# Between passes 3 and 4 of a two-layer forward and backward kernel: the last wq product in one piece ahead of the w2 rows, and the store of x4 moved to the last pass

## The chip, the cores and the metric

The kernel runs on one core of a Trainium2 chip. The metric is device time of one launch in microseconds (us), the median of several runs. One more execution was recorded by the hardware profiler; times inside the kernel come from that record and count from the start of its span. PE is TensorE (PEld its weight loads), DVE is VectorE, ACT is ScalarE, POOL is GpSimd and SP is SyncE, whose queue issues the loads.

## The reference

One token, width 1024, goes through attention over a cache and a dense layer, twice with the same weights; all gradients of it are wanted as well.

```python
x = A_x
x = x + _A_ref(_layernorm(x, axis=-1), A_k_cache, A_v_cache, A_wq, A_wo)   # 32 heads, 4 cache groups, 65536 keys
x = x + _B_ref(_layernorm(x, axis=-1), B_w1, B_b1, B_w2, B_b2)             # relu(h)^2, inner width 3584
x = x + _A_ref(_layernorm(x, axis=-1), A_k_cache, A_v_cache, A_wq, A_wo)
x = x + _B_ref(_layernorm(x, axis=-1), B_w1, B_b1, B_w2, B_b2)
return x
...
_out, _vjp = jax.vjp(_f, A_x, A_k_cache, A_v_cache, A_wq, A_wo, B_w1, B_b1, B_w2, B_b2)
return (_out0, *[jnp.asarray(_g) for _g in _grads])
```

Names in the kernel: L1 and L3 are the two attention layers, L2 and L4 the dense ones; x4 is the result (out_0), and dx3, dx2, dx1 are the gradients on the way back: dx3 at the input of L4, dx2 at the input of L3, dx1 at the input of L2. dq, dO and so on are those inside the attention; dh2 is the gradient at L2's inner width.

## The kernel before

The caches (67 MB each for K and V) are read in four passes: forward of L1, forward of L3, backward of L3 (dq alone), and the last, which does the backward of L1 and writes the gradients of K and V for both layers. A pass goes by cache group and by blocks of 32 x 128 rows, in a pipeline written out step by step; inside passes 1 to 3 the order of PE, DVE and ACT is the written one (`tc.manual_schedule(engines=ORDERED)`), while in pass 4 and in the stage between passes 3 and 4 a scheduler of the language orders the instructions of each engine when the program is built. SP and POOL are ordered by it everywhere.

All loaded blocks, weight slabs and staged outputs live in one arena of 20 slots of 1 MB. A slot is given when it is free by the kernel's own bookkeeping at build time (`take_one`, `Slot`, `give_slot`); at run time a load waits for the last reader of its slot. Loads stand in one SP queue in order. Around the stage in question seven slots keep V blocks for pass 4 and eight keep softmax weights, so five take turns for the weights.

Small work that belongs to a pass runs as background steps (`Background`): urgent ones, such as the row dots of a further wo or wq product (`g_rowdots`, L598 on DVE and L587 on ACT), and normal ones, the outer products of the weight gradients. Normal steps are paced: by step i of the pass, `total * i / steps` are to be done. Pass 4 has some 150 of them.

Between passes 3 and 4 four products follow each other, each of a weight matrix and a vector that the one before gives:

- wq with dq of L3's last group: 8 rows of slabs in two slots; its sum goes into dn3 (L989), through the backward of the layer norm (`ln_bwd`, L248, with a mean over partitions on PE, L212) into dx2 (L1836);
- w2 with dx2: 28 rows in seven 1 MB slabs; it gives dh2 (`fin_dh2`, L1838);
- w1 with dh2: 8 rows of 3584 in eight slabs of 896 KB; it gives dx1 (`fin_dx1`, L1841);
- wo with dx1: 8 rows in two slabs; it gives dOT of L1's first group (`dO_finish`, L946), with which pass 4 starts.

The class `Rows` does such a product. A row of the matrix, 128 x 1024, goes one of two ways, chosen at build time by the running load of the engines. Either PE transposes it in eight pieces (`front`, L682), DVE or ACT copies it out of PSUM (L164 and L161, with `evac` choosing), and eight matmuls multiply it with the vector (`back`, L714); or, for the jobs marked `mix`, DVE multiplies it with the vector spread over the partitions and sums (L673, "row dot"), once that spread vector is there (`bcast_vec`: L535 turns the vector, L537 copies it, L544 spreads it). Jobs marked `inplace` copy the transposed row back over the slab, so that they hold no buffer; the others have six buffers `wt`. `begin` (L639) is called at the first product of a job and needs its vector.

Along with the w2 rows runs x4: each row is also multiplied with the second dense layer's activation (`side_x4`, L1849: eight matmuls L1851 a row into `ps_x4`). After the last row two adds make x4 (L1856, L1857), and `col_to_dram` (L202) turns it on PE (L205), copies it (L207) and stores it from POOL's queue (L208).

`rows.run` (L760) transposes rows until the buffers are full, does the products of an in-place first job, fills again, and then alternates; the wq job is queued first, the w2 job second.

Of the kernel before, what the change touches and what calls it, by code (L numbers as in the profile page):

```python
# [20 lines left out]
def kernel(  # L21
# [25 lines left out]
    D = A_x.shape[-1]  # L47
    G = A_k_cache.shape[1]
# [3 lines left out]
    HQ = QD // DH  # L52
    R = HQ // G
    F = B_w1.shape[1]
    DC, FC = D // P, F // P
# [44 lines left out]
    def ps_mv(shape, dtype=F32):  # L100
        if PS["pass4"]:
            return ps_tr(shape, dtype)
        return PS["pool"].tile(shape, dtype, name="ps_mv", tag="mv", bufs=1)
# [98 lines left out]
    def col_to_dram(col, n, v1d):  # L202
        nj = n // P
        pt = ps_mv([nj, P], F32)
        nc.tensor.transpose(pt[:, :], col[:, :], ident_f[:, :])  # L205
        rows = tmp.tile([nj, P], BF, name="rows_c", tag="rows_c")
        nc.vector.tensor_copy(out=rows[:], in_=pt[:])  # L207
        nc.gpsimd.dma_start(out=v1d.rearrange("(j p) -> j p", p=P), in_=rows[:])  # L208

    def bcast_sum(src, ncols, mean=False):  # L210
        pt = ps_mv([P, ncols], F32)
        nc.tensor.matmul(pt[:, :], lhsT=(onesd_f if mean else ones_f)[:, :], rhs=src, start=True, stop=True)  # L212
        return pt
# [34 lines left out]
    def ln_bwd(dn, n, rstd, between=lambda: None):  # L248
        st = tmp.tile([P, 2], F32, name="lnb_st")
        nc.vector.reduce_sum(out=st[:, 0:1], in_=dn, axis=AX.X)  # L250
        pr = tmp.tile([P, DC], F32, name="lnb_pr")
        nc.vector.tensor_tensor(out=pr[:], in0=dn, in1=n[:], op=ALU.mult)
        nc.vector.reduce_sum(out=st[:, 1:2], in_=pr[:], axis=AX.X)
        between()
        tot = bcast_sum(st[:], 2, mean=True)
        negm = tmp.tile([P, 2], F32, name="lnb_negm")
        nc.vector.tensor_scalar(out=negm[:], in0=tot[:], scalar1=-1.0, scalar2=None, op0=ALU.mult)
        t = tmp.tile([P, DC], F32, name="lnb_t")
        nc.vector.scalar_tensor_tensor(out=t[:], in0=n[:], scalar=negm[:, 1:2], in1=dn, op0=ALU.mult, op1=ALU.add)  # L259
        dx = tmp.tile([P, DC], F32, name="lnb_dx")  # L260
        nc.vector.tensor_scalar(out=dx[:], in0=t[:], scalar1=negm[:, 0:1], scalar2=rstd[:, 0:1], op0=ALU.add, op1=ALU.mult)  # L261
        return dx
# [173 lines left out]
    def d_cols(ap, nb):  # L436
        return ap[:, nb * P:(nb + 1) * P]
# [4 lines left out]
    def f_rows_of(W):  # L442
        return W.rearrange("(s p j) n -> p s j n", p=P, j=4)

    def slabs(name, load, nk, kper, ncols, ahead=1, flat=False):
        pend = deque()
        ks = deque(range(0, nk, kper))

        def fetch():
            k = ks.popleft()  # L450
            i = None
            if ks and flat and NOW["wide"] and not odd_one():
                i = take_pair()
            if i is None:
                kn = min(kper, nk - k)
                sl = Slot(name)
            else:
                kn = min(2 * kper, nk - k)
                ks.popleft()
                sl = Slot(name, at=i, both=True)  # L460
            v = sl.t[:, 0:kn * ncols].rearrange("p (k n) -> p k n", n=ncols)
            nc.sync.dma_start(out=v, in_=load(k, kn))
            pend.append((k, kn, sl, v))

        def gen():
            while ks or pend:
                while ks and len(pend) < ahead:
                    fetch()
                k, kn, sl, v = pend.popleft()
                for kk in range(kn):  # L470
                    NOW["slab"] = sl
                    yield k + kk, v[:, kk, :]
                sl.over = True
                if not sl.users:
                    sl.free()
        g = gen()
        g_fetch = [fetch for _ in range(ahead)]
        return g, g_fetch
# [25 lines left out]
    def w2_slabs(ahead=1):  # L504
        v = f_rows_of(B_w2)
        return slabs("s_w2", lambda k, kn: v[:, k // 4, :, :], FC, 4, D, ahead)
# [105 lines left out]
    class Rows:  # L612
# [147 lines left out]
        def run(self):  # L760
            self.fill()
            first = self.queue[0][0] if self.queue else None
            while first is not None and first["inplace"] and self.queue and self.queue[0][0] is first:
                self.back()
            self.fill()
            while self.queue:
                self.back()
                self.fill()
# [5 lines left out]
    DENSE = {}  # L774
# [99 lines left out]
    def new_layer(name, lay):  # L874
        L = dict(name=name)
        for nm in ("qT", "oT", "rZ", "dOT", "dqT"):
            L[nm] = vec.tile([P, HQ], F32, name=name + "_" + nm)
        L["oTb"] = vec.tile([P, HQ], BF, name=name + "_oTb")
        L["qpad"] = vec.tile([P, G, 8, R], BF, name=name + "_qpad")
        L["negm"] = vec.tile([P, G, NSU, R], F32, name=name + "_negm")  # L880
        L["fw"] = vec.tile([P, G, NSU, R], F32, name=name + "_fw")
        L["nd2"] = vec.tile([64, HQ], BF, name=name + "_nd2")
        nc.gpsimd.memset(L["nd2"][:], 0.0)
        return L
# [24 lines left out]
    def gsl(g):  # L909
        return slice(g * R, (g + 1) * R)  # L910
# [73 lines left out]
    def dn_finish(dn, first):  # L984
        def fin(y):
            if first:
                nc.vector.tensor_copy(out=dn[:], in_=y)
            else:
                nc.vector.tensor_tensor(out=dn[:], in0=dn[:], in1=y, op=ALU.add)  # L989
        return fin  # L990
# [7 lines left out]
    ORDERED = {mybir.EngineType.PE, mybir.EngineType.DVE, mybir.EngineType.Activation}  # L998
# [571 lines left out]
    def n_outer(nA, nB, wide=False):  # L1570
        return -(-nB // 8) + nA // 4 + nA * (-(-nB // 8)) if wide else 1 + nA // 4 * 5
# [14 lines left out]
    L1, L3 = new_layer("L1", 0), new_layer("L3", 1)  # L1586
# [31 lines left out]
    lastg = [ITEMS[p][-1][0] for p in range(4)]  # L1618
    firstg = [ITEMS[p][0][0] for p in range(4)]
    PRE = {}  # L1620
# [7 lines left out]
    bg = Background()  # L1628
# [18 lines left out]
    rows = Rows(DENSE["pool"])  # L1647
# [20 lines left out]
    bg = Background()  # L1668
# [86 lines left out]
    rows = Rows(DENSE["pool"])  # L1755
# [59 lines left out]
    bg = Background()  # L1815
    bg.by_group(2, lambda g: g_dO(L3, dx3, g))

    dn3 = vec.tile([P, DC], F32, name="dn3")
# [10 lines left out]
    dx2 = vec.tile([P, DC], F32, name="dx2")  # L1829
# [2 lines left out]

    def fin_dx2(y):
        dn_finish(dn3, False)(y)
        dxn3 = ln_bwd(dn3[:], L3["n"], L3["rstd"])
        nc.vector.tensor_tensor(out=dx2[:], in0=dx3[:], in1=dxn3[:], op=ALU.add)  # L1836

    def fin_dh2(y):  # L1838
# [2 lines left out]
    def fin_dx1(y):  # L1841
        dxn = ln_bwd(y, L2["n"], L2["rstd"])
        nc.vector.tensor_tensor(out=dx1[:], in0=dx2[:], in1=dxn[:], op=ALU.add)
    rows = Rows(DENSE["pool"])
    rows.add(PRE["wq3"], DC, R, lambda: L3["dqT"][:, gsl(lastg[2])], fin_dx2, inplace=True)
    x4 = vec.tile([P, DC], F32, name="x4")
    ps_x4 = ps_acc([P, DC, 64])

    def side_x4(kc, slab):  # L1849
        for nb in range(DC):  # L1850
            nc.tensor.matmul(ps_x4[:, nb, :], lhsT=d_cols(slab, nb), rhs=L4["gb"][:, kc:kc + 1].to_broadcast([P, 64]),  # L1851
                             start=kc == 0 and nb == 0, stop=kc == FC - 1 and nb == DC - 1, skip_group_check=True)
        add_load(pe=DC * 0.03)
        if kc == FC - 1:
            f = tmp.tile([P, DC], F32, name="ffn_f")
            nc.vector.tensor_tensor(out=f[:], in0=ps_x4[:, :, 0], in1=b2c[:], op=ALU.add)  # L1856
            nc.vector.tensor_tensor(out=x4[:], in0=x3[:], in1=f[:], op=ALU.add)  # L1857
            col_to_dram(x4, D, out_0.rearrange("a b d -> (a b d)"))
    rows.add(w2_slabs()[0], FC, DC, lambda: dx2[:], fin_dh2, mix=True, side=side_x4)
    rows.add(w1_slabs()[0], DC, FC, lambda: dh2[:], fin_dx1, cols=f_cols, mix=True)  # L1860
    rows.add(wo_slabs(firstg[3])[0], R, DC, lambda: dx1[:], dO_finish(L1, firstg[3]), inplace=True)
    rows.run()
# [9 lines left out]
    bg = Background()  # L1872
# [1 line left out]
    bg.normal.append(g_outer(bgpool, out_8, FC, DC, [L4["g"], L2["g"]], [gx, dx2], a_f=True))  # L1874
    bg.normal.append(g_outer(bgpool, out_5, HQ, DC, [L3["oT"], L1["oT"]], [dx3, dx1]))
    bg.normal.append(g_outer_wide(bgpool, out_6, DC, FC, [L4["n"], L2["n"]], [dh4, dh2]))
    bg.total = 2 + n_outer(FC, DC) + n_outer(DC, FC, True) + n_outer(HQ, DC) + (G - 1) * n_outer(DC, DC)
    bg.steps = len(ITEMS[3]) - 4
    dn1 = vec.tile([P, DC], F32, name="dn1")

    def g_biases():
        gb2 = tmp.tile([P, DC], F32, name="gb2")
        nc.vector.tensor_tensor(out=gb2[:], in0=gx[:], in1=dx2[:], op=ALU.add)
        col_to_dram(gb2, D, out_9)
        yield
        gb1 = tmp.tile([P, FC], F32, name="gb1")
        nc.vector.tensor_tensor(out=gb1[:], in0=dh4[:], in1=dh2[:], op=ALU.add)
        col_to_dram_f(gb1, F, out_7)
        yield

    bg.normal.append(g_biases())

    def gwq(g):
        return g_outer(bgpool, out_4, DC, R, [L3["n"], L1["n"]], [L3["dqT"][:, gsl(g)], L1["dqT"][:, gsl(g)]], c0=g * 1024)
# [61 lines left out]
```

## Time and profile before

| | us |
|---|---|
| three runs: median (lowest, highest) | 1941.16 (1941.15, 1943.75) |
| profiled execution, span | 1938.1 |
| busy in the span: PE, PEld, DVE, ACT, POOL | 1585.2, 1301.4, 1170.3, 1044.9, 142.2 |
| DMA: 787.63 MB, mean | 406 GB/s |
| last product of pass 3's K blocks (L1270) begins | 1120.0 |
| last wq product (L714) begins | 1121.9 |
| row dots of w2 (L673), first begins, last ends | 1134.2, 1146.8 |
| dOT of L1's first group (L948) | 1177.5 |

The profiled execution is known by its span, which runs from its first to its last instruction; the runs are timed around the whole launch. A line of a stretch gives its length, then for each engine its busy time and in brackets its instructions, the clock granted to PE (1.00 is full), the busy share of the 16 DMA engines, and what they moved. A line of the order of time gives the start, the length, the engine, the line of the code, the operation, out<-in, shapes and number of instructions merged; in brackets how long the engine had been idle before it and what ended that.

### The profile page before, as it was taken

The page shows a single profiled execution, that of the slowest core. Times are in us where ns is not written, and L with a number is a line of the kernel's source. Part 1 is how long each engine was busy: PE and PEld are TensorE (multiplying, and loading weights), DVE is VectorE, ACT ScalarE, POOL GpSimd, SP SyncE. Part 2 cuts the span into 40 slices and gives each one's busy share as a digit, 9 for nine tenths or more (in the row PEclk, how much of TensorE's full clock was granted, in tenths as well). Part 3 has the DMA queues.
Part 4 walks back from the last instruction along what each step waited for, and adds up shares of the span by engine and source line. Part 5 has one row for each costly group of instructions (what it writes and reads, how often), then busy time and mean ns, then how long its engine had stood idle before and what let it go on. Part 6 is the DMA issues. An engine that isn't in the chain of part 4 may idle for free. (4 is left out here: it accounts for less than half of the span.)

```text
span 1938.1 us, 66986 instructions
## 1 busy us (share of the span) xinstructions
PE 1585.2 (82%) x30199; PEld 1301.4 (67%) x30199; DVE 1170.3 (60%) x2453; ACT 1044.9 (54%) x1617; POOL 142.2 (7%) x321
## 2 busy tenths in 40 slices
PE   6878778688777888977787898889997987697987
PEld 6878777678777877877776886555554654454554
DVE  5655555255555554545454567777775886685876
ACT  3444334245433545445363455766875885575775
POOL 0000000000000000000000001121111211121211
PEclk9999899689999999998899999898997998797998
DMA  9999999999999998999999988999999999899998
GB/s 393 427 425 425 429 427 415 391 407 423 427 425 429 428 422 309 377 425 429 426 424 421 408 314 308 425 424 389 425 424 413 419 424 424 345 419 397 424 422 352
DMA packets 107149, 787.63 MB, mean 406 GB/s; under 512 B 9440, under 2 KB 16622, under 8 KB 42222
## 3 DMA queue, kind: packets, MB, share of 16 engines
q1 hardware_dynamic: 82782, 617.65, 77.2%
q0 software_dynamic: 24080, 165.70, 20.5%
q8 instruction: 236, 3.87, 0.7%
q14 instruction: 51, 0.42, 0.1%
HBM read 617.62 MB, written 165.69 MB: 404 GB/s over the span
## 5 line engine op out<-in xcount | busy, mean ns | idle before, releaser
L164 DVE COPY kt<-ps_tr 128x1024 bf16<-128x1024 bf16 x724 | 496.3, 688 | 429.0 <-PE ps_tr L1024 244.0
L161 ACT CAST arena<-ps_gg 128x1024 bf16<-128x1024 f32 x457 | 444.4, 1011 | 185.0 <-PE ps_gg L1426 137.9
L1024 PE MATMUL ps_tr<-ident_b,arena 128*128 128x128 bf16 x3840 | 308.2, 225 | 36.9 <-DMA arena<-in_A_k_cache_dram 27.5
L161 ACT COPY kt<-ps_tr 128x1024 bf16<-128x1024 bf16 x164 | 171.0, 1046 | 186.1 <-PE ps_tr L1216 103.3
L164 DVE CAST arena<-ps_gg 128x1024 bf16<-128x1024 f32 (+2 forms) x186 | 222.2, 1195 | 77.1 <-PE ps_gg L1426 34.5
L1024 PEld LDWEIGHTS <-arena 128*128 128x128 bf16 x3840 | 232.9, 101 | 44.7 <-DMA arena<-in_A_k_cache_dram 30.3
L1126 PE MATMUL ps_acc<-arena 128*128 128x64 bf16 (+4 forms) x4096 | 205.6, 196 | 60.2 <-DMA arena<-in_A_v_cache_dram 45.1
L1426 PE MATMUL ps_gg<-GG,xt 64*128 64x512 bf16 x1024 | 210.6, 409 | 43.3 <-DVE arena L164 28.3
L1345 PE MATMUL ps_tr<-ident_b,arena 128*128 128x128 bf16 x1824 | 177.4, 232 | 33.7 <-DMA arena<-in_A_v_cache_dram 30.7
L1126 PEld LDWEIGHTS <-arena 128*128 128x128 bf16 x4096 | 159.9, 100 | 66.1 <-DMA arena<-in_A_v_cache_dram 48.7
L1042 PE MATMUL ps_sc<-L_qpad,kt 128*128 128x64 bf16 (+7 forms) x3584 | 183.0, 194 | 16.3 <-issue 8.3
L1107 ACT ACTIVATE arena<-S_sb,L_negm 128x128 bf16<-128x128 f32 x256 | 165.5, 1002 | 55.7 <-DVE L_negm L1092 42.2
L1216 PE MATMUL ps_tr<-ident_b,arena 128*128 128x128 bf16 x1920 | 154.3, 226 | 44.3 <-DMA arena<-in_A_v_cache_dram 43.5
L1345 PEld LDWEIGHTS <-arena 128*128 128x128 bf16 x1824 | 116.8, 103 | 90.7 <-issue 55.2
L1042 PEld LDWEIGHTS <-kt 128*128 128x128 bf16 x3584 | 152.6, 100 | 20.2 <-issue 8.8
L1216 PEld LDWEIGHTS <-arena 128*128 128x128 bf16 x1920 | 117.1, 101 | 48.8 <-DMA arena<-in_A_v_cache_dram 46.1
L1457 PEld LDWEIGHTS <-arena 128*128 128x128 bf16 x2048 | 92.2, 101 | 57.8 <-issue 39.9
L1107 ACT ACTIVATION_READ_ACCUMULATOR arena<-S_sb,L_negm 128x1 f32 x256 | 127.9, 500 | 0.0
L1426 PEld LDWEIGHTS <-xt 64*128 64x128 bf16 x1024 | 64.5, 94 | 90.1 <-issue 52.3
L587 ACT ACTIVATE mv_t<-mv_t 128x1024 bf16<-128x1024 bf16 x96 | 102.1, 1065 | 35.8 <-DVE mv_t L598 35.8
L1382 PE MATMUL ps_sc<-DOB,kt 128*128 128x64 bf16 (+3 forms) x1824 | 112.3, 197 | 0.1
L1270 PE MATMUL ps_acc<-dsT,arena 128*128 128x64 bf16 (+7 forms) x2048 | 103.1, 194 | 11.3 <-DMA arena<-in_A_k_cache_dram 7.8
(317 smaller groups left out, 2154.0 us busy)
## 6 DMA issues: line engine op xcount, KB each, us to landing
arena<-in_A_k_cache_dram SPq DMA_DIRECT2D x82, 2048.0 KB, 21.7
arena<-in_A_v_cache_dram SPq DMA_DIRECT2D x79, 2048.0 KB, 21.7
out_dram<-arena POOLq DMA_DIRECT2D x149, 1024.0 KB, 16.2
arena<-in_A_v_cache_dram SPq DMA_DIRECT2D x84, 1024.0 KB, 14.2
arena<-in_A_k_cache_dram SPq DMA_DIRECT2D x84, 1024.0 KB, 14.6
arena<-in_A_wo_dram SPq DMA_DIRECT2D x22, 1024.0 KB, 19.6
arena<-in_B_w_dram SPq DMA_DIRECT2D x21, 1024.0 KB, 9.2
arena<-in_A_wq_dram SPq DMA_DIRECT2D x18, 1024.0 KB, 18.0
```

What stands on the lines that cost most here:

```text
L161: nc.scalar.copy(out=out, in_=in_)
L164: nc.vector.tensor_copy(out=out, in_=in_)
L587: nc.scalar.activation(out=t[:, :], in_=t[:, :], func=ACTF.Copy, accum_out=y[:, kc:kc + 1])
L1024: nc.tensor.transpose(pt[:, i, :], kb8[:, i, :], ident_b[:, :])
L1042: nc.tensor.matmul(state["ps_s"][:, s:s + w, :].rearrange("p a b -> p (a b)"), lhsT=kt[:, i, :], rhs=L["qpad"][:, g, 0:w, :].rearrange("p ...
L1107: nc.scalar.activation(out=E(p, g, c0, SU)[:, :, h], in_=S[:, h, :], func=ACTF.Exp, bias=L["negm"][:, g, su, h:h + 1], scale=SCALE, accum_ ...
L1126: nc.tensor.matmul(ps_o[:, 0:w, :], lhsT=vb8[:, i, :], rhs=E(p, g, c, w), start=(c % SU == 0), stop=(c % SU == SU - 1), skip_group_check=True)
L1216: nc.tensor.transpose(pt[:, i, :], vb8[:, i, :], ident_b[:, :])
L1270: nc.tensor.matmul(ps_dq[:, 0:w, :].rearrange("p a b -> p (a b)"), lhsT=kb8[:, i, :], rhs=dsT[:, s:s + w, :].rearrange("p a b -> p (a b)") ...
L1345: nc.tensor.transpose(pt[:, i, :], vb8[:, i, :], ident_b[:, :])
L1382: nc.tensor.matmul(state["ps_dp"][:, s:s + w, :].rearrange("p a b -> p (a b)"), lhsT=vt[:, i, :], rhs=DOB[:, g, 0:w, :].rearrange("p a b - ...
L1426: nc.tensor.matmul(pg[:, 512 * h:512 * h + 512], lhsT=xt[64 * h:64 * h + 64, j1 // 8 + m, :], rhs=gg[64 * h:64 * h + 64, :, :].rearrange(" ...
```

## The change

The wq job is no longer queued. Its rows are transposed first; then, in a written order for PE, DVE and ACT, its eight products run together, and the finish `fin_dx2` is called, into which one w2 row is put before the mean on PE and one before the add of dx2; one more follows. The rest of the w2 rows are queued as before. The turning, copying and storing of x4 is taken out of `side_x4` and becomes a normal background step of pass 4, behind those of the bias gradients; the pace counts two steps more.

```diff
     def fin_dx2(y):
         dn_finish(dn3, False)(y)
-        dxn3 = ln_bwd(dn3[:], L3["n"], L3["rstd"])
+        dxn3 = ln_bwd(dn3[:], L3["n"], L3["rstd"], lambda: w2_part(1))
+        w2_part(1)
         nc.vector.tensor_tensor(out=dx2[:], in0=dx3[:], in1=dxn3[:], op=ALU.add)
...
-    rows = Rows(DENSE["pool"])
-    rows.add(PRE["wq3"], DC, R, lambda: L3["dqT"][:, gsl(lastg[2])], fin_dx2, inplace=True)
...
-            col_to_dram(x4, D, out_0.rearrange("a b d -> (a b d)"))
-    rows.add(w2_slabs()[0], FC, DC, lambda: dx2[:], fin_dh2, mix=True, side=side_x4)
+
+    rows = Rows(DENSE["pool"])
+    dn_job = rows.job(DC, R, lambda: L3["dqT"][:, gsl(lastg[2])], fin_dx2)
+    dn_job["inplace"] = True
+    for kc, slab in PRE["wq3"]:
+        run(rows.front(dn_job, kc, slab))
+    w2_rows = w2_slabs()[0]
+    dh_job = rows.job(FC, DC, lambda: dx2[:], fin_dh2, mix=True)
+
+    def w2_part(n):
+        for _ in range(n):
+            kc, slab = next(w2_rows)
+            side_x4(kc, slab)
+            run(rows.front(dh_job, kc, slab))
+    with tc.manual_schedule(engines=ORDERED):
+        rows.begin(dn_job)
+        for _ in range(DC):
+            rows.back()
+        w2_part(1)
+    dh_job["side"] = side_x4
+    rows.jobs.append((w2_rows, dh_job))
...
-    bg.total = 2 + n_outer(FC, DC) + n_outer(DC, FC, True) + n_outer(HQ, DC) + (G - 1) * n_outer(DC, DC)
+    bg.total = 4 + n_outer(FC, DC) + n_outer(DC, FC, True) + n_outer(HQ, DC) + (G - 1) * n_outer(DC, DC)
...
+    def g_out0():
+        yield
+        col_to_dram(x4, D, out_0.rearrange("a b d -> (a b d)"))
+        yield
+
     bg.normal.append(g_biases())
+    bg.normal.append(g_out0())
```

## The prediction

> **What bounds the kernel now.** I read the page first, for the share of each engine and the 40 slices; then the busy time by stretches between 1112 and 1190 us, where pass 3 hands over to pass 4; then the order of time in that stretch, and the waits of the load queue.
>
> ```profile
> span 1938.1 us, 66986 instructions
> DMA  9999999999999998999999988999999999899998
> GB/s 393 427 425 425 429 427 415 391 407 423 427 425 429 428 422 309 377 425 429 426 424 421 408 314 308 425 424 389 425 424 413 419 424 424 345 419 397 424 422 352
> ```
>
> In most slices DMA is full at about 425 GB/s: inside the passes the loads and stores are the bound, and no engine is. The four weakest slices are where one pass hands over to the next: 309 and 377 between passes 2 and 3, 314 and 308 (1114 to 1211 us) here. The page's chain of what ended last covers only the last 1% of the span, so it says nothing of this place.
>
> ```profile
> core 0: us, PE busy (x) PEld busy (x) DVE busy (x) ACT busy (x) POOL busy (x), PEclk, DMA share, GB/s
> 1121.00:1124.00 3.00, 2.12 (x43) 2.06 (x39) 0.67 (x4) 0.00 (x0) 0.00 (x0) 0.57 0.97 352
> 1124.00:1127.00 3.00, 3.00 (x63) 3.00 (x61) 1.26 (x2) 1.01 (x1) 0.00 (x0) 0.86 0.81 333
> 1127.00:1130.00 3.00, 3.00 (x88) 3.00 (x85) 1.24 (x6) 2.02 (x2) 0.00 (x0) 1.00 0.56 180
> 1142.00:1145.00 3.00, 2.92 (x72) 2.61 (x68) 3.00 (x7) 2.22 (x3) 0.00 (x0) 1.00 0.97 354
> 1145.00:1148.00 3.00, 0.85 (x19) 0.78 (x18) 2.41 (x7) 0.89 (x2) 0.00 (x0) 1.00 0.80 273
> 1154.00:1157.00 3.00, 3.00 (x46) 2.57 (x44) 2.95 (x6) 2.58 (x4) 0.00 (x0) 0.76 0.22 89
> 1178.00:1181.00 3.00, 2.69 (x54) 1.87 (x54) 2.30 (x16) 0.63 (x2) 1.04 (x4) 1.00 0.18 30
> ```
>
> Here PE is full from 1124 to 1145 and nearly stops in 1145 to 1148; DVE is full from 1134 on; DMA has holes (0.56, 0.22, 0.18). So the bound is a chain of products, each needing the one before: dx2, dh2, dx1, dOT.
>
> ```profile
> 1121.94 1.84 PE L714 MATMUL ps_bg<-vcb,arena 128*128 128x64 bf16 x31 [0.88 <-DVE vcb L555]
> ...
> 1128.31 1.19 PE L714 MATMUL ps_bg<-vcb,arena 128*128 128x64 bf16 x33
> ...
> 1131.42 0.17 DVE L1836 TENSOR_TENSOR dx<-dx,lnb_dx 128x8 f32<-128x8 f32 x1
> ...
> 1146.81 0.16 DVE L1856 TENSOR_TENSOR ffn_f<-ps_acc,b2c 128x8 f32<-128x8 f32 x1
> ...
> 1147.22 0.27 PE L205 MATMUL ps_mv<-ident_f,x 128*8 128x128 f32 x1 [2.15 <-DVE x L1857]
> ...
> 1151.12 0.18 DVE L732 TENSOR_TENSOR rows_ym<-ps_bg,rows_m 128x28 f32<-128x28 f32 x1
> ...
> 1167.44 1.22 DVE L673 SCALAR_TENSOR_TENSOR mv_junk<-arena 128x1024 bf16<-128x1024 bf16 x1 [1.59 <-DMA arena<-in_B_w_dram]
> ```
>
> The reader is to see two things. The 64 matmuls of the last wq product are split, 31 at 1121.94 and 33 at 1128.31, with six w2 rows between them, so dx2 (L1836) comes at 1131.4. And the transpose of x4 (L205) stands in PE's queue before work that is ready, and waits for an add (L1857) that DVE reaches only after eleven row dots (L673); PE loses 2.3 us.
>
> **The change, part by part.** The built order of the changed kernel shows what the scheduler makes of it: 64 contiguous L714; then six w2 rows (8 matmuls of x4 and 8 transposes each) with the mean of the layer norm's backward (L212) behind the first; three copies of those rows moved on DVE from before the dn3 add (L989) to in and behind the dx2 chain; no L205 there. From the second transition row on, PE's order is the same but for L205.
>
> *The wq product in one piece.* 31 matmuls take until 1123.5, some 52 ns each, at the low clock; this lasts until about 1124.8 (a granted 0.86 of three us leaves 0.84 us at half). By then 25 more are done, and the last 8 at 34 ns (33 in 1.12 us of weight loads at 1128.3) end at 1125.1. L989 starts at 1125.3 and not 1129.54: **-4.2 us**.
>
> *What is given back.* From 1125.1 PE has the six w2 rows ahead of the transpose of dx2 (L535). A pair of 8 and 8 takes 0.69 us (1125.49, 1126.18, 1126.87 in the trace), with L212 some 0.3 more: L535 at 1129.5 against 1131.64. DVE meanwhile does the three copies of 0.69 us; one stands before dx2's add, the last ends at 1129.8, when the transposed dx2 is there. From this row on (L537) the trace needs 2.26 us to the first row dot, of which 0.69 is a copy that now comes behind it: the first dot starts at 1131.45 against 1134.21. Then a copy (0.69) and ten dots of 1.145 us: the eleven end at 1144.9 against 1146.9, **-2.0 us**.
>
> *L205 out of the queue.* PE is by then 0.7 us ahead (its rows at 1135.10 come at 1134.4), and the 2.3 us before L205 are gone. What stands between that stall and the last w2 product are transposes and products of 0.42 and 0.27 us and ACT's copies of 1.01 us, one per 1.19 us of PE: ACT keeps pace. So L732, with dh2, comes 0.7 + 2.3 = **3.0 us** earlier, at 1148.1. Bounds: 2.0 if PE's gain is eaten by copies and only that of the dots is left, 4.2 if all of the first step is kept. I take 3.0, since PE, not DVE, ends last before L732 (a DVE copy waited 2.70 us for PE at 1150.51).
>
> *Behind dh2.* The last three w1 loads are issued at 1156.6 to 1160.4, when transposes behind dh2's broadcast free their slots (DMA share 0.22), and the row dots wait for them at 1167.4; the two wo loads follow, then dx1, dOT and pass 4. All hang on dh2, so all shift by 3.0. Two w2 loads also go out sooner, at 1123.6 and 1125.2 for 1127.1 and 1128.6 (they need the wq slots, free with the product); this fills the hole of 1127 to 1130, but nobody waited for them, and I count nothing.
>
> The trace shows the granted clock at 1.00 through the stall at 1145 and at 0.76 and 0.67 in 1154 to 1160, so the slow rows come nine us later, behind the broadcast of dh2. [...]
>
> *Entry of pass 4.* The V load into slot 3 now stands ahead of the first wo load in SP's queue and is freed by K products that PE does earlier. In the trace DMA is at 66 and 107 GB/s in 1195 to 1197 and 1199 to 1201, SP waits 14.2 us for wo's slot, and this V load goes at 1205.6. One MB at 424 GB/s is 2.5 us: the gain is 0 to 2.5. I take half, **-1.2**. The wo load comes some 50 PE rows later, about 2 us; issued at 1202.05, it was used at 1222.2, which covers it.
>
> *The store of x4 in pass 4.* One transpose (0.27), one cast (0.28), one POOL issue (0.53) near 1800 us, where DMA is at 424 GB/s: hidden, at most 1.1. The two added background steps raise the pace by 2 in some 150: nothing by itself, but it shuffles the order.
>
> Sum: -3.0 - 1.2 = -4.2 us on the span. The page's execution has a span of 1938.1; the median of the runs is 3.1 higher, which lies around it. Predicted: 1941.2 - 4.2 = **1937.0 us**.
>
> **The rivals.**
>
> *Absorbed.* Pass 4 is full of DMA at 424 GB/s, and a start 3 us earlier may be spent in its own waits: PE waits 10.73 us at 1628.6 for a V load, 12.17 us at 1677.0. Against it: in those stretches DMA is busy, and bytes asked for sooner end sooner. Time: about 1940, gain 0 to 2.
>
> *A new stall in pass 4, slower.* The row dots of wo and wq (L598) stand in DVE's queue and wait for their slab; all evacuations queue behind them. At 1675.15 one waited 14.0 us, the slab issued at 1655.8; DMA fell to 0.53 and 0.23 in 1670 to 1680, which loses 6.2 us. The place: the second slab of each wo and wq product. It decides if fewer than about 300 PE rows lie between freeing the slot and the first dot. Against it: in the built orders the three short gaps are 314, 136, 248 rows before and 302, 138, 250 after, and no new one is short. With one more such stall and only 2.0 gained: +4.2, 1945.4.
>
> *One stall fewer.* The same price the other way: -4.2 - 6.2, 1930.8.
>
> That the product stays split is excluded by the built order.
>
> **How the numbers follow.** A timing of this kernel tells about 0.2%, 3.9 us, from no change. Forecast (gain of 2.0 to 6.7): 55%, of which 33 are beyond 3.9 us. Absorbed: 20%. New stall: 13%. One fewer: 12%. So faster 33 + 12 = 45%, within 22 + 20 = 42%, slower 13%. The range reaches from 1931.0 to 1945.4, from one stall fewer to one more; the forecast's own is 1934.5 to 1939.2.
>
> **What would show it.** 64 L714 without a break and L989 near 1125.3; first row dot near 1131.5; no idle before L205 and L732 near 1148; the second K load of pass 4 (slot 0, before at 1179.5) near 1176.5; less of a hole at 1195. Wrong if L732 moves by under 2 us, if the stall of PE shows up before another row, or if the stretches of pass 4 differ by a stall of 5 us or more.

## The result, and the profile after

The changed kernel is slower: 1950.72 us (median of ten runs, 1945.09 to 1956.50) against 1943.28 us (ten runs, 1940.47 to 1946.61); the ratio is **1.0041, 95% interval 1.0028 to 1.0053**, so 5 to 10 us where 4.2 us less was forecast. The profiled execution has a span of 1944.1 us, 6.0 more than before.

The page of the changed kernel, its span and the 40 slices:

```profile
span 1944.1 us, 66990 instructions
DMA  9999999999999998999999988999999999999997
GB/s 394 426 427 426 427 429 414 392 407 426 428 424 429 427 424 302 374 427 429 424 426 421 403 326 332 402 396 424 422 423 409 424 424 398 367 423 409 410 422 291
```

The two slices of the changed stage rose from 314 and 308 to 326 and 332: there the change gained. The slices behind them fell (425 and 424 to 402 and 396), and the last from 352 to 291.

The stage itself, by stretches of the changed kernel (columns as in the prediction):

```profile
1124.00:1127.00 3.00, 2.97 (x78) 2.79 (x75) 1.30 (x9) 1.01 (x1) 0.00 (x0) 1.00 0.88 355
1127.00:1130.00 3.00, 3.00 (x74) 2.99 (x70) 2.56 (x9) 1.30 (x2) 0.00 (x0) 1.00 1.00 388
1145.00:1148.00 3.00, 3.00 (x75) 3.00 (x73) 0.15 (x1) 2.83 (x5) 0.00 (x0) 1.00 1.00 361
```

DMA is full in 1127 to 1130 (1.00; 0.56 before), and PE, which had stopped in 1145 to 1148 (0.85), is busy for all three us. The order of time in the changed kernel:

```profile
1122.93 2.15 PE L714 MATMUL ps_bg<-vcb,arena 128*128 128x64 bf16 x64 [0.87 <-DVE vcb L555]
1127.54 0.16 DVE L1837 TENSOR_TENSOR dx<-dx,lnb_dx 128x8 f32<-128x8 f32 x1
1137.27 0.38 PE L1850 MATMUL ps_acc<-L_gb,arena 128*128 128x64 bf16 x7 [0.56 <-issue]
1142.93 0.63 PE L1850 MATMUL ps_acc<-L_gb,arena 128*128 128x64 bf16 x15 [0.76 <-issue]
1144.98 0.17 DVE L1856 TENSOR_TENSOR x<-x,ffn_f 128x8 f32<-128x8 f32 x1
1149.14 0.33 PE L682 MATMUL ps_tr<-ident_b,arena 128*128 128x128 bf16 x3 [0.86 <-issue]
1150.19 0.17 DVE L732 TENSOR_TENSOR rows_ym<-ps_bg,rows_m 128x28 f32<-128x28 f32 x1
```

The 64 matmuls are one piece, dx2 (L1837) comes at 1127.5 for 1131.4, and nothing waits for x4. But PE has three new stops (0.56, 0.76, 0.86 us) that no engine ended ("issue"), 2.18 us together, and dh2 (L732) comes at 1150.19, not at 1148.1.

**Where the time went.** DMA bounds the passes at 425 GB/s, so each stretch can be given its loss: its length less the MB moved in it divided by 425 GB/s. The stretches are cut at the 270th, 290th, 317th and 422nd load of SP's queue in every kernel; in before these are the last K load of pass 3 (1112.9), the K load that the prediction names (1179.5), one at 1327.2 and the last of all (1903.1).

| us lost | passes 1-3 | stage | entry of pass 4 | middle | behind the last load | (length of that) |
|---|---|---|---|---|---|---|
| before | 29.8 | 17.4 | 11.5 | 18.1 | 8.0 | 35.0 |
| changed | 30.3 | 15.3 | 13.7 | 16.5 | 15.1 | 41.8 |

The stage gains 2.1 and the middle 1.6; the entry loses 2.2 and the end **7.1**. The last load is still issued 0.87 us earlier than before (1902.23 for 1903.10): in this pair of profiles all of the 6.0 us, and more, is lost behind it. Stretches of the end, first before, then changed:

```profile
1926.00:1928.00 2.00, 1.13 (x4) 0.19 (x3) 1.30 (x3) 1.50 (x2) 0.94 (x2) 0.74 0.69 287
1928.00:1930.00 2.00, 1.33 (x6) 0.25 (x5) 1.11 (x2) 1.04 (x2) 1.05 (x2) 0.50 0.78 320
```

```profile
1926.00:1928.00 2.00, 2.00 (x41) 2.00 (x39) 0.00 (x0) 0.00 (x0) 0.00 (x0) 0.50 1.00 418
1928.00:1930.00 2.00, 1.22 (x8) 0.23 (x6) 1.33 (x3) 0.74 (x1) 0.00 (x0) 0.50 0.04 12
1930.00:1932.00 2.00, 1.68 (x6) 0.75 (x6) 1.59 (x6) 0.44 (x2) 0.72 (x1) 0.50 0.05 20
```

In 1926 to 1928 of the changed kernel PE alone works, at half the clock, while DVE and ACT stand still; then DMA moves 12 and 20 GB/s, since no store has anything to send. What led there, in the order of time of the changed kernel:

```profile
1910.43 0.23 PE L1457 MATMUL ps_acc<-X,arena 128*128 128x64 bf16 x2 [1.60 <-DMA arena<-in_A_k_cache_dram]
1922.40 0.17 DVE L1194 SCALAR_TENSOR_TENSOR L_dqT<-dqa,L_rZ 128x8 f32<-128x8 f32 x1
1922.75 1.22 DVE L164 CAST arena<-ps_gg 128x1024 bf16<-128x1024 f32 x1
1923.88 0.16 DVE L555 CAST vcb<-L_dqT 128x8 bf16<-128x8 f32 x1
1924.60 3.65 PE L714 MATMUL ps_acc<-vcb,arena 128*128 128x64 bf16 x64
```

PE comes to the last K products 1.60 us before their load has landed. Behind that wait it still has eight matmuls of rank-2 tiles (L1504) to do and is through with them 13.3 us behind the last load; in before they are done by 10.0, with no wait. So the last dq (L1194) comes 20.2 us behind the last load (16.7 before). The vector is then cast behind an evacuation, the last wq product starts behind the rows of the last rank-2 update, 2.2 us behind dq (0.6 before), and runs in one piece at half clock. The order of these instructions is the scheduler's. In before dq, its cast and the product follow each other at once:

```profile
1919.77 0.17 DVE L1194 SCALAR_TENSOR_TENSOR L_dqT<-dqa,L_rZ 128x8 f32<-128x8 f32 x1
1920.12 0.16 DVE L555 CAST vcb<-L_dqT 128x8 bf16<-128x8 f32 x1
1920.34 0.70 PE L714 MATMUL ps_acc<-vcb,arena 128*128 128x64 bf16 x17 [0.21 <-DVE vcb L555]
```

The question for the experiments was which part of the change turned it over, so far from the edit.

### The profile page after: what moved, and what is told of

Same layout as the page of the kernel before. It is cut to its first block, busy times and chain, and to the rows that moved or that the text cites. A ratio compares the mean times of both kernels' runs of the same rounds, so it can differ in the third digit from the quotient of the medians.

```text
span 1944.1 us, 66990 instructions
## 1 busy us (share of the span) xinstructions
PE 1582.2 (81%) x30199; PEld 1296.4 (67%) x30199; DVE 1171.4 (60%) x2452; ACT 1044.4 (54%) x1618; POOL 142.9 (7%) x321
## 3 DMA queue, kind: packets, MB, share of 16 engines
q0 software_dynamic: 24080, 165.70, 20.4%
## 5 line engine op out<-in xcount | busy, mean ns | idle before, releaser
L161 ACT CAST arena<-ps_gg 128x1024 bf16<-128x1024 f32 (+2 forms) x456 | 443.2, 1010 | 178.9 <-PE ps_gg L1426 133.1
L164 DVE CAST arena<-ps_gg 128x1024 bf16<-128x1024 f32 (+1 forms) x187 | 223.9, 1197 | 73.9 <-PE ps_gg L1426 44.7
L1345 PE MATMUL ps_tr<-ident_b,arena 128*128 128x128 bf16 x1824 | 175.7, 230 | 31.8 <-DMA arena<-in_A_v_cache_dram 18.7
L1216 PE MATMUL ps_tr<-ident_b,arena 128*128 128x128 bf16 x1920 | 154.8, 226 | 41.8 <-DMA arena<-in_A_v_cache_dram 40.5
L1042 PEld LDWEIGHTS <-kt 128*128 128x128 bf16 x3584 | 151.3, 100 | 21.9 <-ACT kt L161 11.1
L1457 PE MATMUL ps_acc<-X,arena 128*128 128x64 bf16 (+3 forms) x1536 | 97.1, 198 | 24.5 <-DMA arena<-in_A_k_cache_dram 24.5
```

What stands on the lines that cost most here:

```text
L161: nc.scalar.copy(out=out, in_=in_)
L164: nc.vector.tensor_copy(out=out, in_=in_)
L1042: nc.tensor.matmul(state["ps_s"][:, s:s + w, :].rearrange("p a b -> p (a b)"), lhsT=kt[:, i, :], rhs=L["qpad"][:, g, 0:w, :].rearrange("p ...
L1216: nc.tensor.transpose(pt[:, i, :], vb8[:, i, :], ident_b[:, :])
L1345: nc.tensor.transpose(pt[:, i, :], vb8[:, i, :], ident_b[:, :])
L1457: nc.tensor.matmul(ps_dq[:, 0:w, :].rearrange("p a b -> p (a b)"), lhsT=kb8[:, i, :], rhs=X[:, s:s + w, :].rearrange("p a b -> p (a b)"), ...
```

## The experiments

Theory A: the two added background steps do it, through the pace, not the moved product. Rival B: the written order with its earlier loads and other slots. Rival C: any change of order, no single part. Ratios are to the kernel before, run on the same chip.

**e1: the written order alone** (the store of x4 back in `side_x4`, no `g_out0`):

```diff
             nc.vector.tensor_tensor(out=x4[:], in0=x3[:], in1=f[:], op=ALU.add)
+            col_to_dram(x4, D, out_0.rearrange("a b d -> (a b d)"))
...
-    bg.total = 4 + n_outer(FC, DC) + ...
+    bg.total = 2 + n_outer(FC, DC) + ...
-    bg.normal.append(g_out0())
```

> The wq product in one piece and the written order of the first w2 rows alone; x4 is turned and stored in the transition as before, and the background of pass 4 has its 150 steps as before. Theory A (the loss of the changed kernel sits in the last 35 us of pass 4, where two more background steps shift the order of the last products): PE's built order behind the last K load is that of before (17, 8 and 39 matmuls of the last wq product, started ahead of the rank-2 rows), so no loss at the end; the loads of pass 4 lead those of before by 1 to 2 us, the first L205 wait of some 2 us is back; time 0.5 to 2 us under before. Rival B (the written order itself, with its earlier loads and other slots, brings pass 4 into a worse rhythm): some 6 us over before, as the changed kernel. Rival C (no single part; any change of order in pass 4 moves it by several us): anything within 6 us either way.

Measured 0.9989 (0.9977 to 1.0000), end 35.7 us. As A; B is out.

**e2: the store of x4 moved alone**, on the kernel before (`g_out0` and the 4 added, the product left split).

> The store of x4 moved into pass 4 with its two background steps, alone; the wq product stays split. Theory A: PE's built order at the end is that of the changed kernel (all 64 matmuls of the last wq product in one piece behind the first rank-2 row), so the last 35 us of before take 40 to 42: 4 to 7 us over before, less up to 2 us for the missing L205 wait. Rival B: within 1 us of before or under it. Rival C: anything within 6 us.

Measured 1.0051 (1.0033 to 1.0070), end 39.7 us, with a wait of 1.76 us for the K load. The end is as A said, the time is more (9.9 us for 4 to 7): it lost 6.3 us at the entry too, which A had not said.

**e3: the whole change without the two steps** (`g_out0` gone, `bg.total` back at `2 + ...`):

```diff
         col_to_dram(gb2, D, out_9)
+        col_to_dram(x4, D, out_0.rearrange("a b d -> (a b d)"))
         yield
```

> The whole change, but the store of x4 joins the first step of the biases, so that the background keeps its 150 steps. Theory A: end as before, the lead of 1.7 us of the transition kept in part: 1 to 2.5 us under before and some 7 us under the changed kernel. Rival B: as the changed kernel, some 6 us over before. Rival C: anything within 6 us.

Measured **0.9989 (0.9980 to 0.9997)**, end 35.1 us. Its interval lies, if barely, under the kernel before, and wholly under the changed one's. Its end, in the order of time:

```profile
1921.44 0.17 DVE L1194 SCALAR_TENSOR_TENSOR L_dqT<-dqa,L_rZ 128x8 f32<-128x8 f32 x1
1921.79 0.17 DVE L555 CAST vcb<-L_dqT 128x8 bf16<-128x8 f32 x1
1922.01 0.70 PE L714 MATMUL ps_acc<-vcb,arena 128*128 128x64 bf16 x17 [0.22 <-DVE vcb L555]
```

The product starts 0.57 us behind dq, at full clock, as in before.

**e4: 152 for 150 in the kernel before**, and nothing else (`bg.total = 4 + ...`).

> The kernel before with only the number of background steps raised by two (152 in place of 150, nothing moved or added). Theory A: the end gets a third order (the last wq product starts behind two rank-2 row transposes, in pieces of 3, 14, 11 and 36 matmuls): a price between those of the two others, 0 to 4 us over before, all of it behind the last load. Rival B: no difference. Rival C: anything within 6 us, with the difference ahead of the last load.

Measured 1.0038 (1.0020 to 1.0057), end 40.9 us. A number in a pacing formula costs as much as the whole change, and more than the 0 to 4 us that A gave it. A's place was half right: 4.7 us more are lost at the end, 6.0 at the entry.

**e5: the last product asked for ahead of the rows**, in the changed kernel; **e6**: the same in e3's kernel.

```diff
-            next(PRE["gwq"])
             PRE["rows"].run()
             next(PRE["gwq"])
+            next(PRE["gwq"])
```

> The changed kernel with one line moved at its end: the last wq product is asked for ahead of the two rows (rowb) of the last rank-2 update, not behind them. In the built order vcb then comes right behind dq (L1194) on DVE and the 64 matmuls right behind the last dK products on PE. Theory A1 (of the 6.9 us that the end takes longer, the 1.6 between dq and the first matmul of the last product are the wait behind rowb, and the rest is the K load that comes late and the half clock): the first matmul follows L1194 after some 0.6 us and not 2.2; but the row tiles of the rank-2 update all come behind it, so the end gets 0.5 to 2 us shorter: some 1.0025 to 1.0035 of before. Rival A2 (the end is set by the 8 tiles of the rank-2 update, not by the product): no shorter or up to 2 us longer than that of the changed kernel.

> The same line moved in the kernel whose x4 store joins the first step of the biases (150 steps). There the product starts 0.6 us behind dq already and is broken by 8 matmuls of the rows alone, so A1 expects 0 to 0.5 us shorter (0.998 to 0.999 of before); A2 expects up to 2 us longer, since two of the rank-2 tiles come later.

e5: the product came 0.43 us behind dq, as A1 said, but the end took 43.4 us, for dq itself came 24.4 us behind the last load (a K wait of 2.13 us, then 10.2 us at half clock). The ratio, 1.0024 (1.0010 to 1.0038), overlaps that of the changed kernel, so a gain is not shown: A2 for the length of the end. e6: 0.9982 (0.9969 to 0.9996), end 36.4 us; the ratio overlaps that of e3, so no gain is shown here either, and the end is 1.3 us longer, as A2 said.

**e7: the changed kernel paced as 150** (`bg.total = 2 + ...`, `g_out0` kept).

> The changed kernel, x4's two steps in it, but paced as 150 steps in all. The built order of the end is a fourth one: the last wq product starts early but is broken by the last four dK products. Theory A (the order of the end, as the pace leaves it, decides): no 2 us wait between dq and the first matmul, so an end of 35 to 38 us behind the last load, and 0 to 3 us over before. Rival B' (two more steps cost, however they are paced): as the changed kernel, an end of 40 us and more.

Measured 1.0002 (0.9990 to 1.0014): the time as A expected, the end not: 41.1 us. The entry lost 11.2, as before. So x4's two steps lengthen the end in this profile even when the pace is right: a pass does at most one normal step per item, so each later step comes two items later. That this costs time is not shown, for the ratio overlaps that of e3 (0.9980 to 0.9997).

**e8: 32 transposes of a constant at the start of the changed kernel**, for the stops without a releaser.

```diff
     open_psum(psA_stack, "psA")
+    for _ in range(4):
+        pt = ps_tr()
+        for i in range(8):
+            nc.tensor.transpose(pt[:, i, :], ident_b[:, :], ident_b[:, :])
```

> The changed kernel with 32 transposes of a constant (64 instructions of PE's queue, their result not used) added at its start. [...] The time within 0.3%.

The two stops in its w2 rows (1.13 and 1.59 us) stand at instructions 42433 and 42689 of PE's queue, the very numbers of the changed kernel, and so 64 instructions earlier in the program: they keep their place in the queue, not their rows. One run, 1947.56 us.

**e9: e3 with the pace sped up, no step added** (`bg.steps = len(ITEMS[3]) - 8` for `- 4`); **e10: e3 paced as 149** (`bg.total = 1 + ...`).

> The kernel of e3 (store of x4 in the first step of the biases, 150 steps in all) with its background paced to end 4 items earlier, nothing else; no step is added. In the built order its last 700 PE rows are word for word those of the kernel before with 152 steps (e4). Theory A (the place of the background steps among the products decides, not their number): as e4, 4 to 7 us over before, 6 to 9 over e3, with an end of 39 to 42 us behind the last load. Rival H (two more steps cost time by themselves, or the order matters only together with the split product and the L205 wait of before): as e3, 2 us under before.

> The kernel of e3 paced as 149 steps, so that the background runs slightly later. The built order of the end is that of a fifth kind: four rank-2 tiles and 8 transposes stand behind the last K products' start, the last wq product in one piece behind the rows and a tile. Theory A: an end of 39 to 42 us and 3 to 7 us over before, as with 152, although the steps come later and not earlier. Rival J (only steps that come earlier cost; a slower pace gives the loads more room): as e3 or under it.

e9: 1.0020 (1.0006 to 1.0034), end 41.7 us, entry 17.3 lost: as A at its lower edge; H is out. e10: 0.9991 (0.9980 to 1.0003), a miss. Its end was longer (38.8 us), its entry good (9.6 lost), and its time is that of e3: not every other order costs. What its longer end cost is not seen in the time.

**Which steps.** By the code, step n is due at the first item i with n - 1 < total * i / 252. With 150, steps 4, 7 and 10 fall due at items 6, 11 and 16; urgent steps take items 16 to 19, so step 10 is done at 20. With 152 it is items 5, 10 and **15**: step 10 slips in ahead of the urgent ones. From there to item 71 of 257 nearly every step is early, most by one item, some by more where urgent steps lie between; from item 76 on both are the same again. So e11 and e12, both made from e3, move early steps alone:

```diff
-            while self.normal and self.done < self.total * i / self.steps:
+            while self.normal and self.done < (self.total + 2 * (i < 16)) * i / self.steps:
```

(e11; e12 has `i >= 6`.)

> The kernel of e3 (150 steps) paced as 152 for the first 16 of the 257 items of pass 4 alone: background steps 4, 7 and 10 come 1, 1 and 5 items earlier, and all later steps when they do in e3. In the built order PE's first 1000 rows of pass 4 are those of e9, and its last 6283 rows are those of e3. Theory A' (the early steps cost in two places, each by the order there: some 3 to 7 us more lost between the third K load of pass 4 and 1330 us, and 4 to 7 us more behind the last load): the first loss stays and the second goes, an end of 35 to 36.5 us, and 0 to 4 us over e3. Rival K (the loss at the end is a late effect of the loss at the entry, the loads merely arriving in another phase): the end is as long as in e9, 40 us and more, though its order is that of e3.

> The kernel of e3 paced as 152 from the seventh item on (step 4 where it is in e3, steps 7 and 10 to 38 earlier by 1 to 5 items). In the built order its last 6295 PE rows are those of e9; the first difference to e3 is 270 rows later than that of e9. Theory A': an end of 39 to 42 us, so 3 to 6 us over e3 at least, plus what its entry loses. Rival K: the end goes with the entry; if the entry loses no more than in e3, an end of 35 us.

e11: 1.0032 (1.0021 to 1.0044), entry 16.5 lost (10.9 in e3), end 35.2 us. e12: 1.0022 (1.0013 to 1.0031), entry 15.5, end 40.5 us. The places and lengths are as A' said, and K is out, for e11 enters as badly as e9 and still ends as e3. The price of e11 is a miss: its ratio lies 0.4% over that of e3, some 8 us, where A' gave 0 to 4. Nor are its early steps the three that the expectation names: by the code, once step 10 is ahead of the urgent steps, those up to the 21st (item 34) come early too. What the entry loses, in the order of time of e11, then of the changed kernel:

```profile
1213.38 1.01 ACT L161 CAST arena<-ps_gg 128x1024 bf16<-128x1024 f32 x1 [5.53 <-DMA out_dram<-arena]
1214.44 1.04 PE L1426 MATMUL ps_gg<-GG,xt 64*128 64x512 bf16 x4 [5.16 <-ACT arena L161]
```

```profile
1209.48 1.01 ACT L161 CAST arena<-ps_gg 128x1024 bf16<-128x1024 f32 x1 [5.55 <-DMA out_dram<-arena]
1210.54 1.04 PE L1426 MATMUL ps_gg<-GG,xt 64*128 64x512 bf16 x4 [5.17 <-ACT arena L161]
```

An evacuation waits 5.5 us for a store to leave its slot, and PE waits behind it. This wait, of 4.9 to 6.4 us at 1206 to 1214, is in the changed kernel, e2, e4, e5, e8, e9 and e11, and in none of before, e1, e3, e6, e7 and e10. It is not in e12 either: there PE waits 6.8 and 4.2 us for K loads at 1284 and 1304, and the entry loses nearly as much. Nor is the wait the whole loss: in the 10 us around it (1207.8 to 1217.8) the changed kernel moves 339 GB/s, which loses 2.0 us. More goes at later waits; PE's wait for a K load near 1250 is 5.7 to 6.2 us in e2, e4, e5, e9 and e11, and 3.2 to 4.5 in before, e1, e3, e6, e7 and e10.

All profiles in one table (us lost as above):

| | stage | entry | middle | end | (length) | ratio |
|---|---|---|---|---|---|---|
| e1 order alone | 18.5 | 9.1 | 21.0 | 10.9 | 35.7 | 0.9989 |
| e3 without the steps | 16.6 | 10.9 | 19.4 | 10.2 | 35.1 | 0.9989 |
| e6 e3, product first | 16.9 | 9.8 | 19.8 | 11.2 | 36.4 | 0.9982 |
| e10 149 | 15.0 | 9.6 | 20.4 | 13.8 | 38.8 | 0.9991 |
| e7 changed, as 150 | 16.6 | 11.2 | 19.0 | 13.7 | 41.1 | 1.0002 |
| e2 store alone | 16.4 | 17.8 | 19.5 | 12.1 | 39.7 | 1.0051 |
| e4 152 alone | 18.8 | 17.5 | 17.8 | 12.7 | 40.9 | 1.0038 |
| e5 changed, product first | 14.2 | 17.1 | 15.5 | 17.3 | 43.4 | 1.0024 |
| e8 changed, padded | 15.2 | 14.7 | 18.1 | 18.1 | 45.0 | |
| e9 faster pace | 13.3 | 17.3 | 17.4 | 15.6 | 41.7 | 1.0020 |
| e11 early to item 16 | 16.5 | 16.5 | 20.3 | 10.0 | 35.2 | 1.0032 |
| e12 early from item 7 | 17.3 | 15.5 | 18.7 | 11.9 | 40.5 | 1.0022 |

The kernels with early steps, the changed one among them, lose 13.7 to 17.8 at the entry, the others 9.1 to 11.5. Their ratios part in the same way: 1.0020 to 1.0051 with early steps, 0.9982 to 1.0002 without. Against C, five kernels of different order (e1, e3, e6, e7, e10) agree within 0.2%, and each timed one with early steps lies above them.

The length of the end does not part the ratios. e11 ends as e3 and costs 0.3%, no less than e9 and e12 with ends of 40 us and more; e10 and e7 have long ends and cost nothing clear of noise. Middle and end together lose 29.6 to 36.2 us in every profile but that of before (26.1), with early steps or without, so part of the 7.1 us found above may be one good execution of before. There is one profile of each kernel, and passes 1 to 3, in the same order in all but e8, lose 28.8 to 32.5 us in these thirteen. So it is shown that early background steps cost time; that the longer end costs time is not shown.

## Why the prediction was wrong

Times from here on are taken from the first matmul of the wq product (1121.94 in before, 1122.93 in the changed kernel, whose pass 3 ended 1 us later).

- *The wq product in one piece: right.* L989 came at +2.2 (forecast 3.4, before 7.6): no half clock fell into the product, and the 64 took 2.15 us. Where it did fall in (e3), +3.6. The 1.2 us beyond the forecast are luck: of the ten profiled kernels with both edits, five have +2.2 and five +3.6 or +3.7.
- *What is given back: right.* First dot +8.5 (forecast 9.5, before 12.3), dots end +21.8 (23.0, 24.9).
- *L205 out of the queue: right, but a size off.* dh2 at +27.26 for +29.17 is a gain of 1.9, not 3.0. The stop behind L205 went; 2.18 us of stops that no engine ended came. Over the ten profiled kernels with both edits dh2 came at +25.8 to +27.6, mean 26.9, a gain of 2.3 against the profile of before (e4, with the same stage, has +29.5). On the clock of the span dh2 came only 0.9 us earlier: by either count it is under the 2 us that the prediction named as a sign of being wrong. e1, where L205 stays, gains nothing (+29.13); e2, where it goes alone, gains 1.8. The one-piece product by itself brought no earlier dh2.
- *Behind dh2 all shifts: right.* The K load of 1179.5 came 2.7 us earlier (mean of the ten: 2.5). That this lead reaches the end of the kernel is not shown: e1, whose dh2 came no earlier, has the ratio of e3, which has the lead.
- *The clock: not settled.* Before has half-clock stretches at 1121.41, 1155.54 and 1199.91 (granted 0.50), of 3.41 us each. The changed kernel has none at all from 1110 to 1206, though dh2 is spread as before; e3 has one at 1152.0 and one at 1169.1. Neither the broadcast nor the stall at 1145 alone decides it, and what does is not shown. Of the 44 such stretches in the trace of before and the 43 in that of the changed kernel, all but the last of each measured 3.41 us or two to six times that (6.83 to 20.48).
- *Entry of pass 4, -1.2: wrong.* The V load did go out ahead of wo's, 10.9 us earlier (1194.7 for 1205.6); but five loads on nothing was left of it (1230.8 for 1229.5), and with the waits above the entry lost 2.2 us more than before. The hole did shrink where the V load went out: in the 10 us from 1197.8 DMA loses 0.6 us (3.8 before, from 1199.5). But the stretches just before and behind it lose 1.2 and 2.0 us more, which leaves nothing. Nor does that order come from the product: e3 keeps wo first, e11 has V first.
- *The store of x4 in pass 4: **the step that failed.*** I wrote that the two steps "raise the pace by 2 in some 150: nothing by itself, but it shuffles the order", and counted nothing. Taken out (e3), the change gains 0.1% (0.6 to 3.9 us, the low end of the forecast and below it); put in the pace alone (e4), they cost 0.4%. The term that was put at nothing measured 7.4 us there (3.9 to 11.1): the higher count brings most background steps up to item 71 forward, and each kernel timed with such early steps is slower than before.
- *The rivals.* The one that comes nearest is the new stall in pass 4, slower, which had 13%; the time is above its 1945.4 too. That its price (6.2) was near is luck, for its mechanism was another: not a row dot that waits for its slab, but an evacuation that waits for a store, and K loads that come late. I had looked for short gaps at the slabs of wo and wq, and there indeed none was new. *Absorbed* stays open for the change without the steps: e3's gain of 0.6 to 3.9 us takes in both. *One stall fewer* adds up to 1930.8, where the range has 1931.0. The built order also showed the turned-over end and entry, and I did not read them there.

Open: how the early steps bring the store's slot into ACT's way, or K loads in e12; why the longer ends of e7 and e10 leave no mark on their times, and the short one of e11 neither; and where the upper half of the changed kernel's runs (1952 to 1956) loses, since its profile caught one of 1946.

## What to carry to other kernels

An edit that touches a counter of a pacing rule is an edit of the whole pass: compare the built order at its entry and its end, row by row, before pricing the edit by its instructions. Cut the span at the same loads in both traces and give each stretch its lost DMA time; this shows where a gain may have been given back. Before believing it, see what several kernels with the suspected part have in common and those without it lack: here that was the entry, and not the end that the first pair of profiles showed. A moved small step can go into a step that is there already: that left the pace alone here (e3).

## What was not expected of the hardware

Of all PE idle times over 0.4 us that no engine ended (35 in before, 36.9 us; 37 in the changed kernel, 33.6 us), every one lies at instruction 193 or 194 modulo 256 of PE's queue, each weight load, matmul and semaphore instruction counted as one. The two stops of e8 are at such places too. What PE waits for there is not shown.

In before, 18 stretches of 256 instructions from one such place to the next took PE 4.5 to 5.0 us without the stop at their end; with it they took 5.65 us on average, some 45 instructions per us, and 15 of them had a stop over 0.25 us. Of the 42 that took 6 to 7 us, 1 had such a stop. Where the wait of 2.3 us ahead of L205 went, such stops stand in the w2 rows: three, 2.18 us together, in the changed kernel, and in e1 one of 2.13 us that ended 3.3 us ahead of L205, which then waited for nothing.
